# Scaling a whole key tile in one Pool instruction, with a newly searched order and engine choice

## The chip, the cores and the metric

The kernel runs on one core of a Trainium2 chip. The metric is the device time of one execution in microseconds (us), lower is better. It is about 2.1 us longer than the span of the profile, which runs from the first to the last recorded instruction.

In the text TensorE, DVE (VectorE), ACT (ScalarE) and Pool (GpSimd) are the engines. A program of this kind gives each engine a fixed list of instructions. The engines run their lists side by side; the program makes them wait for each other only where data or a buffer demands it.

## The reference

Two layers, each a linear attention and a gated MLP, both behind a layer norm and both added to x. S = 2048 tokens, D = 512, 32 heads of 16, F = 1376, bf16.

```python
def _A_ref(x, wqkv, w_phi, wo):            # linear attention
    q, k, v = ...                          # x @ wqkv, split into heads
    pk = einsum("bhsd,hdf->bhsf", k, w_phi)          # the same for q
    phi_k = concatenate([softmax(pk), softmax(-pk)], axis=-1)
    kv = einsum("bhsf,bhsd->bhfd", phi_k, v)         # sums over all tokens
    z  = einsum("bhsf->bhf", phi_k)
    o  = einsum("bhqf,bhfd->bhqd", phi_q, kv) / (einsum("bhqf,bhf->bhq", phi_q, z)[..., None] + 1e-6)
    return o.reshape(B, S, D) @ wo
# x = x + A(layernorm(x)); x = x + B(layernorm(x)); and both once more
```

In the names of operations the four parts are counted from 0: layers 0 and 2 are the attentions, 1 and 3 the MLPs.

`kv` sums over all 2048 tokens, so no query of a layer can be finished before every key of it is done. That makes the keys and values of layer 0 a stage of their own, the first 55 us.

## The kernel before

The program is a list of 3976 operations. For each engine a table (`ORDER`, numbers in base 36) gives the order in which it takes them, and `CHOICE` moves an operation to another engine than the one in the code. Both come from a search that plays the program on a model of the chip. The number behind the buffers in a call is the model's duration in ns.

In stage 1 a tile is 128 tokens, 16 tiles in all. For each tile TensorE makes the products, ACT the exponentials `expk` (128 x 1024: both signs, 32 heads, 16 features), and then:

```python
def knorm(self, t, tag):
    ...
    op("dve", lambda e: e.tensor_reduce(k.Zk[...], k.expk[:, t, ...], AX.X, ALU.add), ..., 1215, f"{tag} Zk {t}")
    op("dve", lambda e: e.reciprocal(k.rZk[...], k.Zk[...]), ..., 545, f"{tag} rZk {t}")
    for u in range(2):                                   # two halves of 512
        kv = k.expk[:, t, u * 4:u * 4 + 4, :, :].rearrange("p g s (h f) -> p (g s h) f", f=16)
        self.op2("dve" if t >= NT - 2 and u else "pool", (lambda kv, u: lambda e: e.tensor_tensor(
            kv, kv, k.rZk[:, rb, u * 32:u * 32 + 32].unsqueeze(2).to_broadcast([P, 32, 16]), ALU.mult))(kv, u),
            [...], [r("phik", t, u)], {"pool": 1000, "dve": 690}, f"{tag} phik {t} {u}", 135.0)
```

Called `Zk`, `rZk` and `phik` below. After all tiles TensorE has summed `kv`; DVE multiplies it by a mask into `kvbd`, and the queries can go on. I call the end of the last of these masks the end of stage 1. DVE also normalizes x (`apply`), Pool also scales queries (`phiq`) and does the small powers for the layer norm.

The softmax here doesn't subtract the row's maximum and nothing guards it: scores larger than these inputs give would overflow.

## Time and profile before

| | before |
|---|---|
| time, median of 4 runs | 381.89 us (381.86 to 383.06) |
| span of the profile | 379.8 us |
| matmul work (worked out in the prediction) | 364.5 us |
| gaps between matmuls | 11.2 us |
| end of stage 1 (last mask of layer 0) | 55.60 us |

The busy shares, the slices, the stretches and the chain at the end of stage 1 are shown in the prediction. Here is what it does not show. First the group of the scalings that the change is about, from the page of before: line, engine, operation, output<-inputs, shapes, count | busy us, mean ns | idle time before and what ended it.

```profile
L746 POOL TENSOR_TENSOR expk<-expk,rZk 128x512 bf16<-128x512 bf16 x49 | 51.9, 1080 | 10.5 <-DVE rZk L743 9.5
```

Then the end of stage 1 on the time line of before, Pool first and then DVE: start, length, engine, line, operation, tile, count.

```profile
45.58 6.75 POOL L746 TENSOR_TENSOR expk<-expk,rZk 128x512 bf16<-128x512 bf16 x6
```

```profile
48.77 2.27 DVE L741 TENSOR_REDUCE Zk<-expk 128x64 f32<-128x1024 bf16 x2
50.97 0.95 DVE L743 RECIPROCAL rZk<-Zk 128x64 f32<-128x64 f32 x2
51.84 2.85 DVE L746 TENSOR_TENSOR expk<-expk,rZk 128x512 bf16<-128x512 bf16 x4
54.62 0.98 DVE L788 TENSOR_TENSOR kvbd<-ps,mask 128x136 bf16<-128x136 f32 x4
```

Pool works until 52.33 without a pause. DVE goes straight from one thing to the next.

### The profile page before, as it was taken

The numbers are of one execution on the slowest core, as the hardware profiler recorded it, in microseconds if no ns is written. First come the engines' busy times: TensorE is split into PE (matmuls) and PEld (weight loads), VectorE is DVE, ScalarE is ACT, GpSimd is POOL, SyncE is SP. The second block draws the span as 40 slices with busy tenths as digits, with TensorE's granted clock in tenths as the row PEclk, the third lists the DMA queues.
The fourth block names the chain that finished last, engine by engine and source line by source line (L and its number), as shares of the span: only waits on it lengthen the run. The fifth ranks groups of instructions, "written<-read, shape, count | busy, mean of one in ns | idle before, by whom it ended". The sixth has DMA issues, their size and how long they took to land.

```text
span 379.8 us, 6898 instructions
## 1 busy us (share of the span) xinstructions
PE 368.1 (97%) x2521; PEld 202.4 (53%) x2565; DVE 276.3 (73%) x604; ACT 223.8 (59%) x460; POOL 132.6 (35%) x253
## 2 busy tenths in 40 slices
PE   6999989999999999999999999999999999999997
PEld 4545554877744454445444446577665454445443
DVE  6999998989989565476789989897875761452323
ACT  4899867777624315984676668485644541452560
POOL 7699951022262000254562297323222200010001
PEclk9999999999999999999999999999999999999999
DMA  8731784332434462320300024457553442122102
GB/s 228 182 76 32 131 257 158 88 60 57 79 65 60 97 86 56 69 43 14 63 8 2 2 56 71 87 88 97 73 103 66 103 85 55 26 44 55 43 28 97
DMA packets 87857, 29.33 MB, mean 77 GB/s; under 512 B 79793, under 2 KB 86801, under 8 KB 87825
## 3 DMA queue, kind: packets, MB, share of 16 engines
q1 hardware_dynamic: 84368, 25.86, 34.2%
q10 hardware_dynamic: 3456, 3.05, 2.5%
q8 instruction: 20, 0.33, 0.4%
q14 instruction: 13, 0.10, 0.1%
HBM read 7.91 MB, written 2.10 MB: 26 GB/s over the span
## 4 chain that ended last, share of the span: by engine, by line
PE 80%; DVE 9%; issue 3%; ACT 3%; DMA 2%; POOL 1%; ACTq 1%; DVEq 0%; POOLq 0%
PE ps L953 35%; PE ps L1002 20%; PE ps L722 7%; PE ps L933 7%; PE ps L813 4%; DVE Zk L741 3%; PE ps L979 3%; DVE rZk L743 2%; PE ps L912 2%; DMA wv_p<-in_A_wqkv_dram 1%; PE ps L877 1%; PE ps L778 1%; DMA yT<-ytile 1%; ACT expk L734 1%; DVE ytile L660 1%
## 5 line engine op out<-in xcount | busy, mean ns | idle before, releaser
L953 PE MATMUL ps<-yT,Wgu 128*128 128x512 bf16 (+2 forms) x869 | 150.3, 320 | 0.9
L953 PEld LDWEIGHTS ps<-yT,Wgu 128*128 128x128 bf16 x880 | 77.8, 98 | 60.2 <-ACT gate_sb L955 2.8
L1002 PE MATMUL ps<-Wd,hT 128*128 128x512 bf16 (+3 forms) x357 | 79.5, 373 | 0.3
L955 ACT ACTIVATE gate_sb<-ps 128x512 bf16<-128x512 f32 (+2 forms) x110 | 50.7, 480 | 38.9 <-PE ps L953 32.0
L1002 PEld LDWEIGHTS ps<-Wd,hT 128*128 128x128 bf16 (+1 forms) x363 | 34.7, 98 | 39.2 <-DVE hT L963 0.7
L746 POOL TENSOR_TENSOR expk<-expk,rZk 128x512 bf16<-128x512 bf16 x49 | 51.9, 1080 | 10.5 <-DVE rZk L743 9.5
L961 ACT ACTIVATE expk<-ps 128x512 bf16<-128x512 f32 (+2 forms) x70 | 32.3, 475 | 30.0 <-PE ps L953 24.9
L707 ACT ACTIVATE sq<-x_sb,nmr 128x512 bf16<-128x512 bf16 x48 | 34.6, 720 | 11.2 <-DVE x_sb L684 8.1
L963 DVE TENSOR_TENSOR hT<-gate_sb,expk 128x512 bf16<-128x512 bf16 (+2 forms) x70 | 24.2, 359 | 21.3 <-ACT gate_sb L955 10.6
L741 DVE TENSOR_REDUCE Zk<-expk 128x64 f32<-128x1024 bf16 x32 | 38.0, 1196 | 0.8 <-ACT expk L734 0.6
L1004 DVE SCALAR_TENSOR_TENSOR x_sb<-ps,rstd,x_sb 128x512 bf16<-128x512 f32 (+2 forms) x33 | 23.6, 717 | 18.0 <-PE ps L1002 16.9
L709 POOL TENSOR_SCALAR rv<-rv 128x1 f32<-128x1 f32 x31 | 7.2, 236 | 81.1 <-ACT sq L707 81.1
L933 PE MATMUL ps<-wo_p,oT 128*128 128x512 bf16 x119 | 30.4, 379 | 0.5
L966 DVE TENSOR_TENSOR hT<-gate_sb,ps 128x512 bf16<-128x512 bf16 (+2 forms) x40 | 21.7, 545 | 11.3 <-PE ps L953 4.7
L684 DVE SCALAR_TENSOR_TENSOR x_sb<-ps,x_sb 128x512 bf16<-128x512 f32 x32 | 21.9, 683 | 10.5 <-PE ps L933 6.4
L838 DVE TENSOR_REDUCE Zq<-expq 128x64 f32<-128x1024 bf16 x24 | 28.7, 1198 | 0.2
L846 POOL TENSOR_TENSOR expq<-expq,rho 128x256 bf16<-128x256 bf16 x34 | 20.7, 623 | 22.6 <-DVE rho L843 22.1
L711 POOL TENSOR_TENSOR rstd<-rv,mone 128x1 f32<-128x1 f32 x32 | 17.9, 565 | 25.3 <-DVE rv L709 24.2
L813 PE MATMUL ps<-Wqp,yT 128*128 128x512 bf16 x90 | 22.9, 379 | 0.3
L722 PE MATMUL ps<-Wkp,yT 128*128 128x512 bf16 x85 | 21.8, 379 | 0.7 <-ACT expk L734 0.4
L722 PE MATMUL ps<-wv_p,yT 128*128 128x512 bf16 x83 | 21.7, 379 | 0.5 <-issue 0.2
L700 DVE TENSOR_SCALAR ytile<-x_sb,nmr 128x512 bf16<-128x512 bf16 x48 | 17.4, 366 | 5.3 <-DMA yT<-ytile 4.6
(125 smaller groups left out, 489.4 us busy)
## 6 DMA issues: line engine op xcount, KB each, us to landing
out_dram<-x_sb ACTq DMA_DIRECT2D x15, 128.0 KB, 1.7
x_sb<-in_A_x_dram SPq DMA_DIRECT2D x3, 512.0 KB, 5.6
Wgu<-in_B_W_gate_dram SPq DMA_DIRECT2D x4, 344.0 KB, 4.2
Wgu<-in_B_W_up_dram SPq DMA_DIRECT2D x4, 344.0 KB, 4.2
Wd<-in_B_W_down_dram SPq DMA_DIRECT2D x5, 256.0 KB, 3.4
yT<-ytile SPq DMA_TRANSPOSE x56, 2.5
qT<-expq SPq DMA_TRANSPOSE x40, 2.5
x_sb<-in_A_x_dram SPq DMA_DIRECT2D x4, 128.0 KB, 3.6
```

The lines of the kernel that those rows point to most:

```text
L707: op("act", lambda e: e.activation(k.sq[:], k.x_sb[:, t, :], ACT.Square, scale=-float(D), bias=k.nmr[:, t, :], accum_out=k.rv1[:, t, :]), ...
L722: op("pe", (lambda ic, bank, W: lambda e: e.matmul(k.pb[bank][:], k.yT[:, ic, t * 128:(t + 1) * 128], W[:, ic, :], start=(ic == 0), stop=( ...
L741: op("dve", lambda e: e.tensor_reduce(k.Zk[:, zb, :], k.expk[:, t, :, :, :].rearrange("p g s (h f) -> p (g s h) f", f=16), AX.X, ALU.add), ...
L746: self.op2("dve" if t >= NT - 2 and u else "pool", (lambda kv, u: lambda e: e.tensor_tensor(kv, kv, k.rZk[:, rb, u * 32:u * 32 + 32].unsqu ...
L813: op("pe", (lambda ic, bank, tt: lambda e: e.matmul(k.pb[bank][:], k.yT[:, ic, tt * 128:(tt + 1) * 128], k.Wqp[:, ic, :], start=(ic == 0), ...
L838: op("dve", lambda e: e.tensor_reduce(k.Zq[:, b, :], k.expq[:, t, :, :, :].rearrange("p g s (h f) -> p (g s h) f", f=16), AX.X, ALU.add), ...
L933: op("pe", (lambda c, bank: lambda e: e.matmul(k.pb[bank][:], k.oT[:, ob, c, :], k.wo_p[:, c, :], start=(c == 0), stop=(c == NC - 1)))(c, ...
L953: op("pe", (lambda bank, W, ic, fc, Mf: lambda e: e.matmul(k.pb[bank][0:Mf, 0:n], W[:, ic, fc * 128:fc * 128 + Mf], k.yT[:, ic, c0:c0 + n] ...
L955: op("act", (lambda Mf, gb, gs: lambda e: e.activation(k.gate_sb[0:Mf, gs, 0:n], k.pb[gb][0:Mf, 0:n], ACT.Relu))(Mf, gb, gs), [self.RP[gb] ...
L961: op("act", (lambda Mf, ub, up: lambda e: e.activation(up[0:Mf, 0:n], k.pb[ub][0:Mf, 0:n], ACT.Copy))(Mf, ub, up), [self.RP[ub]], ru, 170 ...
L963: op("dve", (lambda Mf, up, gs, u: lambda e: e.tensor_tensor(k.hT[0:Mf, u, 0:n], k.gate_sb[0:Mf, gs, 0:n], up[0:Mf, 0:n], ALU.mult))(Mf, u ...
L1002: op("pe", (lambda fc, Kf, u, c0, bank, m0, m1: lambda e: e.matmul(k.pb[bank][:, m0:m1], k.hT[0:Kf, u, c0:c0 + 128], k.Wd[0:Kf, fc, m0:m1] ...
```

## The change

Intent: where both halves of a layer 0 key tile are on Pool, scale them in one instruction and pay the fixed cost of an instruction once. Beside it the durations in the model are corrected, and order and engines come from a new search, in which transfers land with more noise. The search is free to change everything else too.

```diff
 ORDER = { ... }                       # all five tables differ (100 lines each, cut)
 CHOICE ...                            # about 105 operations change engine (cut)
@@ def knorm(self, t, tag):
+        eu = [CHOICE.get(f"{tag} phik {t} {u}", "dve" if t >= NT - 2 and u else "pool") for u in range(2)]
+        if tag == "A0" and eu == ["pool", "pool"]:
+            kv = k.expk[:, t, :, :, :].rearrange("p g s (h f) -> p (g s h) f", f=16)
+            op("pool", lambda e: e.tensor_tensor(kv, kv, k.rZk[:, rb, :].unsqueeze(2).to_broadcast([P, 64, 16]), ALU.mult),
+               [r("expk", t, 0), r("expk", t, 1), r("rZk", rb)], [r("phik", t, 0), r("phik", t, 1)], 1930, f"{tag} phik {t} 0")
+            return
         for u in range(2):
 ...
-                ..., {"pool": 1000, "dve": 690}, f"{tag} phik {t} {u}", 135.0)
+                ..., {"pool": 1053, "dve": 683}, f"{tag} phik {t} {u}", 135.0)
```

Thirteen of the 16 tiles are merged, so the program has 13 operations fewer.

## The prediction

> **What bounds the kernel now.** I read the busy shares first, then the 40 slices, the stretches, the chain of waits, and last the groups.
>
> ```profile
> PE 368.1 (97%) x2521; PEld 202.4 (53%) x2565; DVE 276.3 (73%) x604; ACT 223.8 (59%) x460; POOL 132.6 (35%) x253
> ...
> DVE  6999998989989565476789989897875761452323
> ...
> POOL 7699951022262000254562297323222200010001
> ```
>
> TensorE is the bound over the whole span. A busy share of 97% does not say how much can be won, so I counted its work. There is one weight load per matmul, 2565 in all, which is complete where the matmul records (2521) are not. Spacing comes from unbroken runs in the chain: 11 matmuls of 512 columns take 2.38 us, that is 216 ns each; 20 of 256 columns take 2.19 us, about 108 ns; single starts give 55 ns for 128 columns, 84 for 192, 63 for 144, 33 for 68. By the program's shapes that is 1333 x 0.216 + 240 x 0.1085 + 337 x 0.055 + 128 x 0.084 + 64 x 0.063 + 448 x 0.033 + 2.3 for a few odd ones = 364.5 us. The span is 379.8 us, so only 15.3 us are not matmul work. The first matmul starts 1.6 us in, and 2.6 us pass after the last starts. The remaining 11.2 us are gaps. Summing start-to-start minus the spacing above by stretch gives 5.0 us of gaps in 0 to 20, 0.5 in 20 to 40, 2.9 in 40 to 60, 1.0 in 60 to 80 and 1.9 in all the 300 us from 80 to the end. The largest single gaps there are 0.6 us at 155.8 (behind a transposing transfer that fetched yT, in the chain from 146.1) and 0.6 us at 241.4.
>
> ```profile
> 20.00:40.00 20.00, 19.70 (x135) 9.75 (x136) 19.74 (x27) 19.94 (x29) 19.75 (x26) 1.00 0.28 55
> 40.00:55.60 15.60, 14.41 (x141) 8.12 (x141) 15.56 (x24) 12.45 (x20) 12.33 (x15) 1.00 0.88 193
> ...
> 80.00:380.00 300.00, 294.69 (x1875) 158.29 (x1905) 203.34 (x463) 161.45 (x351) 84.47 (x162) 1.00 0.32 60
> ```
>
> The columns after the length are PE, PEld, DVE, ACT, POOL busy with counts, then clock and DMA. From 20 to 55.6 us DVE has no slack at all and Pool has none until it ends its last key scaling at 52.3. TensorE meanwhile lives on projections that need neither, and runs short of them only from 49 us. The chain shows what it then waits for:
>
> ```profile
> 51.04 0.87 DVE rZk L743 x2
> 51.91 2.78 DVE expk L746 x4
> 54.69 0.91 DVE kvbd L788 x4
> ...
> 58.65 1.90 PE ps L859 x8
> ```
>
> The four scalings at L746 are tiles 14 and 15, both halves on DVE. So the end of the first stage is DVE's sum (Zk), reciprocal (rZk), scaling, mask: DVE ends it, Pool is 2.3 us ahead. This is the only place where the change can reach the bound, and at most about 3 us of gaps lie there.
>
> **What the Trainium skill says.** "Perfetto Trace Analysis", section Identifying the Most-Contended Engine, says that matmul busy share is a bad measure of headroom because matmuls are pipelined. This trace agrees: a 512-column matmul is listed with 379 ns and starts every 216. Its section GPSIMD Engine Instruction says that Pool instructions should be timed by the spacing of their starts, not by the reported duration; here the reported median is 1054 ns and five in a row take 5.15 us, so a start every 1.01 to 1.03. "GPSIMD Engine Reference", section Key points, says that Pool shares its SBUF interfaces with VectorE and contends with DVE instructions in a two-port mode or with two SBUF inputs. The trace shows how: such a DVE instruction stands until the Pool instruction under way is over.
>
> ```profile
> 34.26 5.15 POOL L746 TENSOR_TENSOR expk<-expk,rZk 128x512 bf16<-128x512 bf16 x5
> ...
> 36.27 1.22 DVE L660 TENSOR_SCALAR ytile<-x_sb,rstd,nmr 128x512 bf16<-128x512 bf16 x1
> ```
>
> The same DVE instruction takes 0.40 us when undisturbed; this one began just after a Pool scaling and ended 0.16 us after that scaling did. The reductions and reciprocals beside the same Pool work are not stretched.
>
> **The change part by part.** (1) For layer 0, 13 of 16 tiles have both halves on Pool. Each such pair becomes one 1024-element instruction, so 13 instructions go. From the trace, 512 elements take 1.05 us and 256 (the query scaling) 0.62, a slope of 0.43 per 256 and a fixed part of 0.19. A whole tile is then 0.19 + 4 x 0.43 = 1.91 us, with a spacing 0.04 shorter, 1.87 against 2 x 1.01 = 2.02. Saved: 0.15 us a tile, 13 x 0.15 = 2.0 us of Pool by 52 us (2.2 if the longer form has no surprise in it, nothing if the slope steepens). This lies beside DVE's chain, not on it. What it can give TensorE is the 0.6 us in which the key-value sum of tile 11 waited for Pool at 49.4, and the first half of each tile comes about 0.9 us later than before, which takes some of that back.
>
> (2) Engines before the first key-value result. I summed the durations of the kernel before over both orders, up to the last mask of the key-value product. DVE had 54.1 us and gets 53.6: the zeroing of a buffer goes to Pool (0.54, but in the idle time before the first statistics, so worth nothing), one normalization goes to ACT (-0.40) and one weight evacuation comes from ACT (+0.42). From the first statistics on, DVE has the same work to within 0.1 us. ACT grows by 0.2 us.
>
> (3) Port waits on DVE. In the kernel before, eight two-port or two-input DVE instructions in 18 to 53 us stand 0, 0.30, 0.14, 0.29, 0.82, 0.67, 0.17 and 0.37 us longer than undisturbed, 2.8 us in all: these lie on the binding chain. With Pool instructions of 1.9 us in place of 1.05, a wait of random phase doubles. There are seven of them in the new order, and an order search that knows this cost will place them close to the end of a Pool instruction. An estimate: 3.3 us, that is +0.5, give or take 1.5.
>
> (4) Later engine swaps. About 105 small operations change sides, mostly between DVE and Pool in layer 2, nearly balanced (for layer 2 keys: 6 to Pool, 12 to DVE). In 160 to 260 us DVE is 18% idle and TensorE loses 1 us there, so these cost or give at most a few tenths. An order chosen against noisier transfers should place the yT transposes earlier: I give it 0.6 of the 1.9 us of gaps after 80.
>
> (5) The start. ACT loads its table after two DMA issues instead of six, so four weight transfers are issued some 1.3 us later, and the x transfers have the queues to themselves a little more. DVE could begin its statistics earlier, TensorE its first V product later. I put this at 0, give or take 0.7.
>
> The sum: Pool's part -0.3, port waits +0.5, later gaps -0.6, start 0, and -0.2 for a better fit of the last DVE scalings to TensorE's leftover work = -0.6 us. 381.9 - 0.6 = 381.3 us.
>
> **The rivals.** *The Pool saving goes straight through.* If Pool were the last link at 52 us, 2 us less Pool would be 2 us less time: 379.9. For it speaks Pool's full 20 us stretch and the wait at 49.4; against it that the chain there names DVE in every piece from 47.7 to 58.2 but for issue time, and that no DVE work moves to the relieved Pool in this stage. *DVE pays for the longer Pool instructions.* If each of seven exposed instructions waits 1 us, the chain is 7 - 2.8 = 4 us longer, and since TensorE has little left to do from 49 us, most of it arrives: up to 385. For it speaks the 1.22 us case; against it that an order with known costs avoids bad phases, as before's average of 0.35 us does. *The start decides.* Gaps of 5.0 us there are the largest pool; a late weight or a hole in DVE before its first key reduction (17.3 us) would shift everything by 1 us either way: 380.5 or 382.5. *A transfer in the middle lands late* and holds TensorE for 1 to 2 us; the reordered queue has 171 transfers' worth of chances, but before shows only one gap of that kind, 0.6 us.
>
> **Range and chances.** TensorE's 364.5 us, the 1.6 and 2.6 at the ends and the 2.1 us by which the median exceeds the span are a floor of 370.8. To be 2% faster (374.3) the gaps would have to shrink from 11.2 to 3.5 us, though 5.0 lie in a start that waits for the first loads. To be 2% slower (389.5) they would have to grow by 7.6. Neither fits any part above. The parts' spreads (1.5, 0.7, 0.5) combine to about 1.7 us, so 379.6 to 382.9 for 8 in 10. Chances: 0.01 faster, 0.985 within 2%, 0.005 slower.
>
> **What would show it right or wrong.** Pool: 13 key scalings of 128x1024, starting 1.85 to 1.95 us apart; above 2.0 means part 1 saved nothing. DVE: the last layer 0 mask should end within 1 us of 55.6, and the exposed instructions should sum to 2 to 5 us of stretch; the chain in 48 to 58 us should still name DVE. TensorE: the same 2565 weight loads, and gaps after 80 us of 1 to 2 us. I am wrong if the 40 to 60 stretch loses over 5 us or under 1, or if a chain piece of a transfer over 2 us appears that was not there.

## The result and the profile after

| | before | after |
|---|---|---|
| time, median of 4 runs | 381.89 us (381.86 to 383.06) | 379.52 us (379.34 to 380.30) |
| span of the profile | 379.8 us | 377.4 us |
| gaps between matmuls | 11.2 us | 8.8 us |
| end of stage 1 | 55.60 us | 54.05 us |
| first key sum (`Zk` of tile 0) begins | 17.32 us | 16.31 us |
| Pool's last key scaling of stage 1 ends | 52.33 us | 51.39 us |
| port standing on DVE in stage 1 (explained below) | 2.69 us | 1.11 us |

The ratio is 0.9934, with a 95% interval of 0.9911 to 0.9958. A ratio here is the mean time of one kernel's runs over that of the other's of the same rounds, so it is not quite the ratio of the medians quoted. Within 2%, as predicted, but four times the predicted 0.6 us and just below the predicted range (379.6 to 382.9). All outputs are right.

"Port standing" is what the last row is about, and it is used in all experiments. It is the sum, over three kinds of DVE instruction of stage 1, of the time each took beyond the undisturbed one: 0.40 us for a normalization, 0.68 for a half-tile scaling, 0.43 for a query scaling. It is taken from DVE's time line against Pool's, as in the prediction's example (1.22 instead of 0.40 us). What the traces show is that such an instruction, begun under a Pool instruction, ends a fixed time after that one, however long that was; that a shared port is the reason is taken from the page cited in the prediction.

The page of after: busy shares and slices, then the merged group.

```profile
PE 367.7 (97%) x2519; PEld 203.9 (54%) x2565; DVE 276.2 (73%) x607; ACT 227.0 (60%) x463; POOL 130.8 (35%) x234
...
DVE  5999998989968676459799999898984654342323
...
POOL 6799941133344001350463577023221201000020
...
L750 POOL TENSOR_TENSOR expk<-expk,rZk 128x1024 bf16<-128x1024 bf16 x13 | 25.9, 2005 | 0.6 <-DVE rZk L746 0.6
```

The work is the same: 2565 weight loads, TensorE at 97%. Only the gaps are fewer. The spread of one line's durations (lowest/median/highest ns, then when) shows what one instruction costs, after and before:

```profile
L750 POOL TENSOR_TENSOR expk<-expk,rZk x13: 1925/1929/2377, 18.5 to 49.0; 128x1024 bf16<-128x1024 bf16 x13
```

```profile
L746 POOL TENSOR_TENSOR expk<-expk,rZk x49: 1047/1054/1504, 19.5 to 237.1; 128x512 bf16<-128x512 bf16 x49
```

A whole tile takes 1.93 us, and three in a row take 5.75 us, so they start every 1.91 us. Two halves start 1.01 to 1.02 us apart, 2.02 to 2.04 together. Saved: 0.11 to 0.13 us a tile by the spacing, 1.4 to 1.7 us for 13 tiles. (The durations of Pool's layer 0 key scalings sum to 29.18 us before and 27.12 after, 2.06 less; neighbours overlap a little in the trace, and without the overlap it is 1.5 us less.) The highest value in each line is 0.45 us above the median. There a DVE scaling had begun ahead of it (at 47.54 us in before, 48.84 in after), and Pool stands behind DVE: the delay goes both ways.

The stretches of after, to be read against those of before in the prediction (length, then PE, PEld, DVE, ACT, POOL busy with counts, clock, DMA, GB/s):

```profile
20.00:40.00 20.00, 19.84 (x146) 10.25 (x148) 19.87 (x29) 19.70 (x28) 19.51 (x22) 1.00 0.33 64
40.00:54.10 14.10, 13.79 (x130) 7.63 (x129) 13.96 (x23) 12.59 (x20) 11.32 (x9) 1.00 1.00 217
```

DVE is still full to the end of stage 1, and that end comes 1.55 us earlier. The chain of waits just before it (start, length, what):

```profile
43.02 2.36 POOL expk L750
...
45.47 2.00 POOL expk L750
47.46 0.58 POOL expq L855
48.04 1.02 POOL expk L755
...
49.53 1.22 DVE Zk L744
...
50.77 0.55 DVE rZk L746
51.32 1.83 DVE expk L755 x3
```

Up to 49.1 us the chain now names Pool, then DVE. Its shares over the whole span, of before and of after:

```profile
PE 80%; DVE 9%; issue 3%; ACT 3%; DMA 2%; POOL 1%; ACTq 1%; DVEq 0%; POOLq 0%
```

```profile
PE 85%; POOL 7%; DVE 3%; issue 2%; ACT 1%; DMA 1%; POOLq 0%; DVEq 0%
```

Pool's share went from 1% to 7% although it has less to do: the engine that the chain names can change while the two remain coupled. And the end on the time lines of after:

```profile
49.02 2.38 POOL L750 TENSOR_TENSOR expk<-expk,rZk 128x1024 bf16<-128x1024 bf16 x1
```

```profile
49.53 1.21 DVE L744 TENSOR_REDUCE Zk<-expk 128x64 f32<-128x1024 bf16 x1
50.77 0.55 DVE L746 RECIPROCAL rZk<-Zk 128x64 f32<-128x64 f32 x1
51.24 1.91 DVE L755 TENSOR_TENSOR expk<-expk,rZk 128x512 bf16<-128x512 bf16 x3
53.07 0.98 DVE L797 TENSOR_TENSOR kvbd<-ps,mask 128x136 bf16<-128x136 f32 x4
```

Pool is over at 51.39, just as DVE begins its last three scalings, and these take 1.91 us, 0.64 each: nothing stands. In before Pool was in the way of the first of DVE's four (until 52.33).

Where did the 2.4 us of span come from? I laid both traces side by side by the amount of matmul work done. After is ahead by 1.55 us once the first stage's work is done, by another 0.25 us from 80 to 100 us and by 0.6 us at before's 155.8, where a transfer held before up. The gaps of the start itself (0 to 20 us) are 0.17 us larger than before, although the first key sum comes 1.0 us earlier: two statistics were moved behind it, so DVE merely does the same work in another order. Lengths counted from the first key sum therefore compare only kernels with the same start: after does 1.28 us more of statistics in that stretch than before.

### The profile page after: what moved, and what is told of

Read it like the earlier page. It is cut to its first block, busy times and chain, and to the rows that moved or that the text cites. A ratio compares the mean times of both kernels' runs of the same rounds, so it can differ in the third digit from the quotient of the medians.

```text
span 377.4 us, 6882 instructions
## 1 busy us (share of the span) xinstructions
PE 367.7 (97%) x2519; PEld 203.9 (54%) x2565; DVE 276.2 (73%) x607; ACT 227.0 (60%) x463; POOL 130.8 (35%) x234
## 4 chain that ended last, share of the span: by engine, by line
PE 85%; POOL 7%; DVE 3%; issue 2%; ACT 1%; DMA 1%; POOLq 0%; DVEq 0%
PE ps L962 37%; PE ps L1011 20%; PE ps L725 7%; PE ps L942 7%; POOL expk L750 5%; PE ps L822 5%; PE ps L988 3%; PE ps L921 2%; PE ps L787 1%; PE ps L886 1%; DMA hT<-in_A_wqkv_dram 1%; DVE Zk L744 1%; POOL rstd L648 1%; PE ps L868 1%; PE ps L539 0%
## 5 line engine op out<-in xcount | busy, mean ns | idle before, releaser
L1011 PE MATMUL ps<-Wd,hT 128*128 128x512 bf16 (+4 forms) x354 | 79.3, 373 | 0.5
L855 POOL TENSOR_TENSOR expq<-expq,rho 128x256 bf16<-128x256 bf16 x36 | 22.2, 624 | 24.4 <-DVE rho L852 23.7
L750 POOL TENSOR_TENSOR expk<-expk,rZk 128x1024 bf16<-128x1024 bf16 x13 | 25.9, 2005 | 0.6 <-DVE rZk L746 0.6
L755 POOL TENSOR_TENSOR expk<-expk,rZk 128x512 bf16<-128x512 bf16 x17 | 19.1, 1134 | 11.8 <-DVE rZk L746 11.5
L712 POOL TENSOR_SCALAR rv<-rv 128x1 f32<-128x1 f32 x22 | 4.3, 203 | 45.3 <-ACT sq L710 45.3
```

The lines of the kernel that those rows point to most:

```text
L750: op("pool", lambda e: e.tensor_tensor(kv, kv, k.rZk[:, rb, :].unsqueeze(2).to_broadcast([P, 64, 16]), ALU.mult), [r("expk", t, 0), r("exp ...
L1011: op("pe", (lambda fc, Kf, u, c0, bank, m0, m1: lambda e: e.matmul(k.pb[bank][:, m0:m1], k.hT[0:Kf, u, c0:c0 + 128], k.Wd[0:Kf, fc, m0:m1] ...
```

## The experiments

The first theory, *Pool on the chain*: in stage 1 DVE and Pool are both full and hold each other up at the shared port, so Pool's work is as much on the path as DVE's, and saving Pool time saves time. (In the expectations R1 goes by Pool's work, P by the phases in which DVE meets Pool, and PR joins the two.) A rival, *the order*: DVE's chain binds, longer Pool instructions mean longer waits if anything, and the new order only happens to place DVE's exposed instructions in better phases. A second rival, *the tail*: the gain lies in later transfers that land better. There were three calls of four kernels; each call was on another chip, with 11 runs of before in it: medians 382.85, 382.75 and 381.96 us.

### Parts of the change alone

**e1: after, but with halves.** All of the new order and engines, the merge undone.

```diff
-        if tag == "A0" and eu == ["pool", "pool"]:
+        if False:
# Pool's order: each merged operation followed by the second half
```

> The changed kernel, with its engines and its order, but each of the 13 whole-tile Pool scalings is two half-tile ones again, one behind the other. In the two profiles the last layer 0 mask on DVE ends at 55.60 us before and at 54.06 us after (1.54 earlier), the DVE instructions that share ports with Pool stand 2.77 us longer than undisturbed before and 1.21 after (1.56 less), and Pool ends its last layer 0 key scaling at 52.33 before and 51.40 after. Theory P (the gain of the first stage is the shorter standing of DVE behind Pool): the mask ends at 54.06 plus whatever the standing sums to beyond 1.21; with halves no single wait is over 1.1 us, so the sum is 1 to 3 and the time 379.5 to 381.3, moving with that sum. Rival R1 (the gain is the 2 us of Pool work saved): Pool ends 1.9 us later, the gain of the first stage is lost whatever DVE's waits are, time 381.0 to 381.5.

Measured: ratio 0.9981 (0.9954 to 1.0009), 382.32 us. Stage 1 ends at 55.63, as in before; port standing 3.03 us. The end on the time line, Pool and then DVE:

```profile
49.59 3.98 POOL L760 TENSOR_TENSOR expk<-expk,rZk 128x512 bf16<-128x512 bf16 x3
```

```profile
51.82 2.91 DVE L760 TENSOR_TENSOR expk<-expk,rZk 128x512 bf16<-128x512 bf16 x3
```

DVE's same three scalings take 2.91 instead of 1.91 us, because Pool is at its own until 53.57. From 44 us on TensorE waits for no Pool instruction here, but 1.4 us for DVE scalings. The new order without the merge has lost the whole gain of the first stage. P and R1 both had the stage end later, so e1 does not tell them apart, and its time lies above the ranges of both. (Most of this kernel's runs had a mean granted clock of 0.995; its one run at 1.0 took 382.37 us, so the clock is not the reason.)

**e2: before, with the merge.** The merged block put into before's program, before's order and engines untouched, each merged operation at the place of its later half.

> The kernel before, order and engines untouched, but the 13 pairs of Pool key scalings of layer 0 become whole-tile ones, each at the place of the later of its two halves. P: the order was not chosen for instructions of 1.9 us, so DVE's standing behind Pool grows from 2.77 to 3 to 5 us, the mask ends as much later than 55.6 and the time is 382 to 384. R1: Pool ends 1.9 us earlier, the wait of the tile 11 key-value sum (0.77 us) goes, time 380.4 to 381.2.

Measured: ratio 0.9981 (0.9949 to 1.0014), 381.79 us. P's expectation that the waits grow with the longer instructions was a miss: port standing fell to 1.64 us. R1's time was a miss too: Pool ended at 52.22, only 0.11 us sooner. The stage began late (first key sum at 17.94 us) and ended at 56.05; from the first key sum to its end it was 38.11 us long against 38.28 in before, which has the same start. So the merge alone gives at most a fraction. Its order was not made for it: Pool idled 0.83 us for a DVE statistic at 24.7, TensorE waited 1.2 us (0.6 in before) for a whole tile at 50.3, whose first half now came later, and a hole of 0.45 us opened before the masks, which wait for TensorE. That later first half is the cost that the prediction named in step 1.

**e5 and e6: head and tail.** Order and engines of one kernel up to about 60 us, of the other from there: e5 has after's first stage with before's rest, e6 the reverse.

```diff
# at about 60 us of the program's own start times: ORDER[e] = head of one + rest of the other, CHOICE likewise (99 and 98 entries)
```

> Engines and order of the changed kernel for every operation that it starts in about the first 61 us, engines and order of the kernel before for all later ones. By the matmul gaps of the two profiles 1.55 us of the 2.4 us are gained by then. P and R1: 1.5 us below before, 380.1 to 380.7, with the mask at 54.1. Rival R2 (the gain is the later order, fitted to transfers that land late): 381.3 to 382.

> The reverse: the kernel before up to about 62 us, the changed kernel's engines and order for everything later. P and R1: only the later 0.85 us are gained (the 0.59 us gap before the second unit of the third slab, which in before ends at 155.8 behind a transfer, is gone), 380.8 to 381.4, mask at 55.6. R2: 379.6 to 380.3.

Measured: e5 0.9941 (0.9909 to 0.9973), 380.98 us; e6 0.9963 (0.9935 to 0.9990), 381.61 us. Stage 1 ends at 54.07 and 56.03. Both parts count: neither interval reaches 1. Both times are misses by 0.2 to 0.3 us, each above the range of P and R1. The intervals are wide because before itself scatters in these rounds from 381.86 to 384.75. By the fastest run of each the head is worth 2.2 us (381.86 to 379.63) and the tail 0.7 (381.15); but the 2.2 rest on one run, and with e5's next (380.65) it is 1.2. The tail alone is out as the cause; how the gain splits is better read from the profiles (1.55 and 0.85 us).

**h4: after once more**, unchanged, on the third chip.

> The changed kernel unaltered, once more, beside the others: ratio 0.9934 as in its first timing, 0.992 to 0.995; its own runs within 1 us of each other, where runs of the kernel before spread over 2 to 3 us.

Measured: ratio 0.9927 (0.9905 to 0.9950), 379.57 us; stage 1 ends at 53.95, port standing 1.08 us. The result repeats.

### Is Pool on the chain?

**e7: after, with 2 us more of Pool work.** Two extra Pool multiplications into a scratch buffer that nothing needs then, ahead of the scaling of tile 13.

```diff
+        if tag == "A0" and t == 13:
+            for _ in range(2):      # 512 elements each, ident * ident -> k.sq
+                op("pool", lambda e: e.tensor_tensor(k.sq viewed as [P, 4, 128], ident, ident, ALU.mult), ...)   # shortened
```

> The changed kernel with 2 us of useless Pool work (two 512-element products on a scratch) put in front of the last key scaling on Pool, tile 13: the 2 us that merging saved are given back at one place, without moving the phases before it. R1: Pool ends its key scaling at 53.4, the last DVE scalings collide with it, most of the 2 us come back: mask 1.0 to 2.0 us later, ratio 0.997 to 0.999. P alone (only the phases before 50 us matter): mask at most 0.4 later, ratio below 0.995.

Measured: ratio 0.9983 (0.9964 to 1.0001), 381.58 us, about 2 us slower than after. From the first key sum to its end the stage grew by 1.94 us, and port standing grew from 1.11 to 3.03 us. Pool, then DVE:

```profile
48.56 2.60 POOL L752 TENSOR_TENSOR sq<-ident 128x512 bf16<-128x512 bf16 x2
51.12 2.37 POOL L759 TENSOR_TENSOR expk<-expk,rZk 128x1024 bf16<-128x1024 bf16 x1
```

```profile
50.78 3.87 DVE L764 TENSOR_TENSOR expk<-expk,rZk 128x512 bf16<-128x512 bf16 x3
```

DVE's last three scalings take 3.87 us for 1.91: the second of them stands 1.73 us behind Pool's last. Nothing needed the result of the added work. So at this place in after's order Pool's time is on the path one for one. DVE does not pause before the masks, so it reaches the end of the stage inside the length of DVE's own instructions. TensorE also waited 1.6 us for Pool directly, for the delayed tile 13, so the loss of time alone would not tell the two ways apart; e1, where TensorE did not wait for Pool there and the stage ended as late, does. With e1 this is the test that decides between Pool on the chain and the order alone. (Four of the six runs had a granted clock of 0.995 or 0.996; the two at 1.0 took 381.16 and 381.57 us.)

### Can an order alone avoid the waits?

**e3: before, one swap.** DVE's reciprocal of tile 8 put behind the normalization of tile 13, a swap that moves the two longest stands off a Pool instruction (0.82 and 0.67 us), by a count over the trace of before.

```diff
- ... A0 rZk 8, L0 apply 13 ...      (DVE's order)
+ ... L0 apply 13, A0 rZk 8 ...
```

> The kernel before with two neighbours on DVE exchanged: the normalization of tile 13 goes ahead of the reciprocal of key tile 8; Pool untouched. By the trace of before the normalization then starts at 35.8 us instead of 36.3, 0.5 us before the Pool scaling under way ends at 36.3 instead of just after the next one began, and stands 0.26 instead of 0.82 us; the query scaling of tile 1 moves 0.56 us earlier and stands 0.2 instead of 0.67. P: DVE's standing falls from 2.7 to about 1.7 us, the time from the first key sum to the last mask from 38.3 to about 37.3, the kernel is 0.5 to 1.0 us faster (ratio 0.9974 to 0.9987). R1 (Pool's work decides): nothing changes, ratio 1.000.

Measured: ratio 0.9988 (0.9969 to 1.0006), 381.94 us. The two stands fell as worked out, to 0.28 and 0.25 us. But the sum is 2.61 us, as good as unchanged, and stage 1 ends at 55.73:

```profile
46.05 7.02 POOL L752 TENSOR_TENSOR expk<-expk,rZk 128x512 bf16<-128x512 bf16 x6
```

```profile
51.10 3.72 DVE L752 TENSOR_TENSOR expk<-expk,rZk 128x512 bf16<-128x512 bf16 x4
```

DVE came to its last four scalings 0.74 us earlier and stood there 0.86 us longer than in before, since Pool was busy until 53.07. The wait removed in the middle came back at the end. (The ratio does not decide: its interval holds both expectations.)

**e4: after, one swap that should do harm.** A query scaling on DVE put ahead of the reciprocal of tile 12.

> The changed kernel with two neighbours on DVE exchanged: the scaling of query tile 1 goes ahead of the reciprocal of key tile 12, so it starts 0.5 us earlier while Pool is still at tile 10 and should stand about 0.5 us longer. P: DVE's standing 1.1 to 1.6 us, the last mask 0.45 us later (37.75 to 38.2 from the first key sum), ratio to before 0.9945 instead of 0.9934. R1: no change, 0.993.

Measured: ratio 0.9940 (0.9924 to 0.9956), 380.11 us. The query scaling stood 0.59 us longer and the scaling at 49.2 us stood 0.42 us; stage 1 ended 0.7 us later (0.45 was expected), at 54.73, where three profiles with after's own first stage (after, h4, e5) lie within 53.95 to 54.07. So by the profile the order counts as well: a bad phase costs several tenths that Pool's work did not force. In the ratio e4 and after are not told apart.

### Later stages

**e8: before, the late transfer of layer 2 moved.** In before TensorE stopped 0.6 us at 155.8 us. The chain there, and the DVE instruction at its beginning with its wait in brackets:

```profile
146.13 3.41 DMA yT<-ytile
...
154.93 0.69 ACT expk L734
155.62 0.14 issue
155.75 1.02 PE ps L722 x4
```

```profile
149.56 0.35 DVE L700 TENSOR_SCALAR ytile<-x_sb,nmr 128x512 bf16<-128x512 bf16 x1 [2.07 <-DMA yT<-ytile]
```

DVE waits 2.07 us for a transfer to release its buffer. In e8 that normalization and its transfer go behind the last ones of layer 1.

```diff
- L2 apply 1 / L2 tr 1 ahead of L1 apply 15 / L1 tr 15
+ L2 apply 1 / L2 tr 1 behind them
```

> The kernel before with one normalization of the third layer (tile 1) and its transposing transfer moved behind those of tiles 14 and 15 of the layer before, as in the changed kernel. In before DVE stood 2.07 us at 149.6 for the transfer that frees that buffer, and TensorE lost 0.59 us at 155.8. If the later gain is the order fitted to late transfers: this gap goes, 0.5 to 0.7 us faster (ratio 0.998 to 0.9987). If that gap has another cause (ACT's own queue): it stays.

Measured: in the profile DVE's wait for the transfer is gone there, and with it the gap (0.5 to 0.6 us less). The time says nothing: ratio 1.0000 (0.9977 to 1.0023), 382.17 us, six runs from 381.43 to 384.09. The local cause is shown; its worth in time is not resolved.

### Is there something better?

For three kernels I searched the order of the first stage again, by exchanges of neighbours, on the model with Pool's durations and the start taken from the traces. Engines were kept.

```diff
# h1: before.  h2: before with the merge.  h3: after.
# ORDER of the first ~95 entries of DVE, Pool and ACT and ~700 of TensorE replaced
```

> The kernel before, its engines and its half-tile Pool scalings kept; only the order on each engine in the first 60 us is searched anew, with the Pool durations of the traces (1.05 us a half tile where the program says 1.00; 1.03 for a power over four tiles where it says 0.63) and the start of the trace. P (the order's fit alone gives the gain of the first stage): the mask moves 1.5 us earlier, ratio 0.996. PR (standing and Pool work are two ends of one rope: without the 2 us of Pool work saved an order can give little): mask about 0.6 earlier, ratio 0.998 to 0.999.

> The same search for the kernel before with merged key scalings (the merged kernel that in its old order ended its mask at 38.1 us after the first key sum, against 38.3 before). PR: merging and an order made for it give together what neither gives alone, mask 1.3 us earlier than the kernel before of the same start, ratio 0.996 to 0.997 (the later stages stay before's). P: the same as the half-tile kernel searched anew, 0.998 to 0.999. R1: as the merged one in its old order, 0.998.

> The changed kernel, its engines kept, with the same search for its first 60 us. PR: 0.5 us earlier mask, about 53.5, and 0.3 to 0.5 us less time than the changed kernel run beside it.

| | ratio to before | median us | first key sum | port standing | end of stage 1 |
|---|---|---|---|---|---|
| h1, halves | 0.9987 (0.9962 to 1.0012) | 381.60 | 17.34 | 2.42 | 55.31 |
| h2, merged | 0.9981 (0.9956 to 1.0007) | 381.50 | 18.21 | 1.07 | 55.36 |
| h3, after | 0.9957 (0.9933 to 0.9982) | 380.64 | 16.52 | 1.88 | 55.40 |

h3 was a miss: the model had it ahead of after, and it was 1.1 us slower (a hole of 0.93 us ahead of the key sum of tile 8, a stand of 1.24 us behind Pool). h2 was a miss too: 0.996 to 0.997 was expected. Its way from first key sum to the end is 37.15 us, 1.1 shorter than in before (with one normalization, 0.4 us, moved ahead of it), but it begins late and lost 0.8 and 0.5 us at later transfers in its profile, so its time does not show it. In h1 the mask came 0.3 us sooner than in before, less than either theory said; its ratio fits the second (PR). No kernel here beats the changed one; it is the best version I have.

### All of stage 1 in one view

| kernels | Pool's key scalings of stage 1 | port standing, us |
|---|---|---|
| before, e1, e3, e6, e8, h1 | halves | 2.69, 3.03, 2.61, 2.69, 2.72, 2.42 |
| after, h4, e5, e2, h2, h3, e4 | merged, 1.5 to 2 us less | 1.11, 1.08, 1.07, 1.64, 1.07, 1.88, 1.99 |
| e7 | merged, and 2 us more of other work | 3.03 |

What DVE does in stage 1 apart from standing and from holes was 47.9 to 48.8 us in every one of these kernels. The standing sorts by how much scaling and padding Pool has to do, not by how long one Pool instruction is. Within each row the order makes up to 0.9 us of difference. Little standing is not yet an early end: e2 and h2 lost it again in holes of DVE (0.9 and 0.8 us against 0.3 in before).

## Why the prediction was wrong

- **The bound and the class: right.** TensorE with 364.5 us of work in both, so the change could only reach gaps, and "within 2%" had to hold.
- **Step 1, Pool's duration: right, its saving somewhat high; its place: wrong.** A whole tile was put at 1.91 us and took 1.93, 13 instructions went; 2.0 us were to be saved, 1.4 to 1.7 were. The failing sentence is "This lies beside DVE's chain, not on it", with -0.3 in the sum. In e7, 2 us of Pool work with no consumer cost about 2 us; in e1, undoing the merge in after's order put the end of stage 1 back by 1.58 us. So in after's order the Pool saving lay on the chain nearly whole. In before's order it did not (e2).
- **Step 3, port waits: wrong in sign.** Predicted 3.3 us (+0.5), from the assumption that a wait of random phase doubles with the instruction's length; measured 1.1 us (-1.58). Its own expected band of 2 to 5 us failed. The phases are not random: DVE's last scalings come after Pool's last ones or stand behind them, so the sum follows Pool's work (table above). Steps 1 and 3 are thus largely one term, counted twice with opposite signs. Together with step 5 and the -0.2 for fit the sum for the first stage was 0.0; measured -1.55. This is the error.
- **Step 2, DVE's work: right.** No relief there, none seen.
- **Step 4, later gaps: mechanism right for the 0.6 us at 155.8 (e8), size somewhat low.** Predicted -0.6; 0.85 in the profile of after, about 0.4 in that of h4 (span less the end of stage 1, against before). In the mean time of many runs e6 shows 0.37% (1.4 us, with 0.1% to 0.65% as its interval), more than the profile, because before has long runs: 13 of the 33 lay above 383.0 us, against a lowest of 381.27. After's ten runs all lie within 379.06 to 380.30. What makes before's long runs was not caught in a profile of before: in kernels with before's later stages gaps of 0.8 to 1.2 us behind late transposing transfers appear in some profiles (e2 at 101 us, e5 at 245), at different places. TensorE's gaps after 80 us sum to some 1.9 to 3.4 us in the six profiles with before's later stages unaltered (before, e2, e3, e5, h1, h2) and to 1.1 to 1.8 in the seven with after's. That these are the same cause as the long runs is likely, not shown.
- **Step 5, the start: right.** Predicted 0 give or take 0.7; +0.17 us of gaps.
- **What it said would show it wrong.** The last mask "within 1 us of 55.6": it ended at 54.05, so this failed. "The chain in 48 to 58 us should still name DVE": from 49.1 us on it names DVE, with 0.7 us of TensorE at 53.7, but what leads up to it is now Pool. The other signs held: starts 1.91 us apart, the same weight loads, gaps after 80 us within or near 1 to 2; past the start no transfer over 2 us is on the chain (at the start one of 2.95 us took the place of one of 4.48).
- **Small slips in its sums.** The matmul work as written adds up to 364.4 us, not 364.5, which changes nothing.

The rival that came closest was the first, "the Pool saving goes straight through": 379.9 against a measured 379.52. It was turned down because the chain named DVE in every piece from 47.7 us. That was the misreading: the chain names the engine whose instruction was running, and 2.7 us of DVE's instructions in the stage were spent standing behind Pool. The prediction had measured these itself (2.8 us) and still called Pool off the path. The closeness of its number is partly luck: it has 2 us from Pool, where the profile has 1.55 us from the first stage and 0.85 from later ones.

Neither part brings the gain of stage 1 by itself: the merge in the old order made the stage 0.17 us shorter from its first sum (e2), the new order with halves ended it no sooner (e1), both together 1.55 us sooner. One reason the old order profits little is in its model: it had a half tile at 1.00 us where the trace has 1.05, and the power for four tiles at 0.63 where the trace has 1.03, so by an estimate Pool ran 1.6 to 2.0 us behind the plan by 38 us (16 half tiles, two or three powers) and the phases that the search chose were missed. After's program was made with 1.93 us for the whole tile, which is what the trace shows. This reason fits the traces, but h1, which re-searched the old program with corrected durations, gained only 0.3 us in the stage, so it is at most a part.

## What to carry to other kernels

If two engines hold each other up and both are full, the time of either can be on the path, whatever engine the chain of waits names: compare each instruction's length with its undisturbed one before calling the other engine free, and pad the other engine by a known amount to see. Here a wait removed by reordering alone came back elsewhere (e3), and work cut without a new order was mostly lost in other waits (e2). Judge a new order by the spread of its runs as well as by one profile.

## What the Trainium skill lacked or had wrong

- "GPSIMD Engine Reference", section Key points, names the contention of Pool and DVE but no size. (That the later of the two is blocked for the whole instruction of the other is not lacking: it stands in "SBUF — State Buffer".) What no page has is what these traces add: a DVE instruction begun under a Pool instruction ends 0.15 us (normalization), 0.28 us (query scaling) or 0.55 us (half-tile scaling) after it, and stood up to 1.73 us (e7); and Pool stood some 0.45 us behind a DVE half-tile scaling (1.50 for 1.05 us, 2.38 for 1.93). Reductions and reciprocals were not stretched. That a cost of this kind appears as busy time of the waiting engine, and under that engine's name in the chain, is on no page that I read.
- "GPSIMD Engine Reference", section 3.1, gives about 2.6 cycles for an element of a two-input Pool operation in fp32. That would be an estimated 2.2 us for 1024 elements at the 1.2 GHz it uses, before any fixed cost. In bf16 with a broadcast second input, 512 more elements cost 0.88 us here (1.93 less 1.05), 1.7 ns or 2.1 cycles an element, fixed part 0.17 us.
- "Perfetto Trace Analysis", section GPSIMD Engine Instruction, calls the listed duration of a Pool instruction unreliable. Here it was not far off: three whole tiles take 5.75 us, a start every 1.91 us for a listed 1.93.
- "TensorE: Matmul & The Clock Gate", section Back-to-back issue gap, says that a sustained stream of weight loads and matmuls of 512 columns runs at about 131 ns each and calls 216 ns the isolated figure. In this kernel, with a weight load for every matmul and a granted clock of 1.00, 11 in a row take 2.38 us, 216 ns each; 128 columns take 55 to 56 ns where the page says 81.
